# Dividing by the softmax sum after the product with v for eight tiles, with the sums from TensorE, and a new order of the first stage

## The chip, the cores and the metric

The kernel runs on one core of one Trainium2 chip. The metric is the device time of one execution in microseconds (us), as the median of three runs. Engines are called by the profile's names: PE is TensorE's matmul side and PEld its weight loads, DVE is VectorE, ACT is ScalarE, POOL is GpSimd, SP is SyncE, which issues nearly all DMAs.

## What is computed

Attention inside chunks of 64 tokens, for 8 batches of 8 heads, 576 tokens and 64 elements per head, then two feed-forward blocks over the 4608 tokens:

```python
scores = scale * np.matmul(q_c, k_c.transpose(0, 1, 2, 4, 3))     # q_c, k_c, v_c: chunks of 64 tokens
scores = scores - np.max(scores, axis=-1, keepdims=True)
attn = np.exp(scores)
attn = attn / (np.sum(attn, axis=-1, keepdims=True) + 1e-09)
out = np.matmul(attn, v_c)
...
xn = x / rms * rms_g                       # x: 4608 tokens x 512
g = xn @ w_gate                            # 512 x 1536
silu = g * (1.0 / (1.0 + np.exp(-g)))
val = xn @ w_val
x = silu * val @ w_out                     # 1536 x 512
h = x @ w_in                               # 512 x 2048
out = (h * np.cos(h)) @ w_out              # 2048 x 512
```

## The kernel before

The program has four stages: attention with the first four blocks of 128 gate and value columns, the other gate and value columns, the first output product with the second block's first product, and the last product. From the second stage on a product of blocks is made from seven smaller ones; nothing of that is touched. All large products run in three passes on values split into a high half and a low half (`mm3`, line 293).

The change is in the first stage. It takes 36 tiles of 128 tokens (all 8 heads of two chunks), two tiles to a unit. What each engine does, in which order, is written out by hand as a string of step names, `ORDER`; an engine executes its own steps in exactly the order of the string and waits where a step's input or buffer isn't there yet. The first letter names the step and the number the tile (or the unit, for s and v):

- s (sx for the second tile): PE makes the scores of a unit, 32 products on 64x64 quarters of the array, line 401 or 418. m: DVE takes row maxima (433, 435). b: DVE subtracts them (447, 450). e: ACT takes the exponential in place (454).
- n: DVE sums the rows (459), adds 1e-9 (460) and takes the reciprocal (461). z: the tile is multiplied by it (469), by POOL for tiles 0 and 1 as a step of its own, by DVE at the end of n for all others.
- t: PE transposes the tile (476). c: ACT copies it to SBUF (481). v: PE multiplies by v for a unit (492), again 32 products on 64x64 quarters, with the transposed tile as the weights.
- r: ACT sums squares (506). w: POOL makes the factor (511, 513). y: DVE scales (517). x: PE transposes (525). j: ACT makes the high half (534). a: ACT copies (539). l: the low half, by POOL for tiles 0 and 1 (545), by DVE for others (547).
- D: SP loads a block of gate or value weights, which come as 64-bit floats. k (ACT), p and q (DVE, lines 122, 123 and 127, 128), H (ACT) and L (POOL) turn it into high and low halves; k20 is block 2 of the gate weights, k21 of the value weights. Steps with a leading P do the same for weights of the second stage.
- gA2: the gate product of token chunk A (256 tokens, tiles 0 and 1; B is tiles 2 and 3) with weight block 2, 12 matmuls of 256 columns; vA2 the value product; S is ACT's silu, h DVE's multiplication, Y the store.

PSUM has eight banks: four under the tag `at` (scores, transposed tiles, product with v), in turn, and four under `gv` (gate and value products, and the scores of units 1 and 3). A step that takes a bank waits until the readers of the step four banks back in that ring are through.

Of the kernel before, what the change touches and what calls it, by code (L numbers as in the profile page):

```python
# [9 lines left out]
F32 = mybir.dt.float32  # L10
# [10 lines left out]
P = 128  # L21
# [19 lines left out]
POOL_Z = 2  # L41
POOL_L = 2
# [40 lines left out]
def kernel(  # L83
# [275 lines left out]
    with ExitStack() as st:  # L359
# [10 lines left out]
        unit, pair = {}, {}  # L370

        def load_qk(n):
            t = wp.tile([P, 2, NHP, P], F32, tag=f"p{22 + n % 4}", name="qk")
            nc.sync.dma_start(out=t, in_=qk[n])
            unit[n] = {"qk": t}

        def load_v(n):

            vt = ap_.tile([P, D], F32, tag="v", name="v", bufs=4)
            if n % 2:  # L380
                nc.sync.dma_start(out=vt[HD:, :], in_=v[n * P : n * P + HD, :])
                nc.sync.dma_start(out=vt[:HD, :], in_=v[n * P + HD : (n + 1) * P, :])
            else:
                nc.sync.dma_start(out=vt, in_=v[n * P : (n + 1) * P, :])
            unit[n]["v"] = vt
# [70 lines left out]
        def unit_n(n):  # L456
            p = unit[n]["p"]
# [8 lines left out]
        def unit_z(n):  # L466
            p, z = unit[n]["p"], unit[n].pop("z")
# [15 lines left out]
        def att_v(u):  # L483
            for b in range(2):
                unit[u + b]["o"] = bank("o")
            for hp in range(NHP):
                for h in range(2):
                    for b in range(2):
                        s = unit[u + b]
                        for c in range(2):  # L490
# [7 lines left out]
                            )  # L498
            for b in range(2):
                unit[u + b].pop("pts"), unit[u + b].pop("v")  # L500

        def unit_r(n):
# [3 lines left out]
            nc.scalar.activation(s["xn"], s["o"], AF.Square, accum_out=s["ss"])  # L506
# [143 lines left out]
        def step(name):  # L650
# [19 lines left out]
            D00 Q0 s0 k00 p00 Q1 q00 m0 Q2 Q3 sx V0 b0 H00 e0 I Pl0 s1 V1 m1 b1 e1 n0 n1 L00 z0 t0 D01 m2 Pa0 z1 m3 c0 b2 b3  # L670
            Q4 Dg e2 t1 Pb0 c1 Q5 D20 k01 e3 v0 V2 r1 n2 r0 w1 p01 n3 y1 w0 V3 t2 t3 c2 y0 s2 q01 Pc0 c3 k20 m4 D21 Q6 x0 m5
            a0 j0 b4 Pd0 e4 b5 x1 n4 l0 v1 e5 j1 a1 Q7 r3 n5 r2 t4 w3 V4 Pl1 V5 t5 w2 c5 p20 D31 Pa1 k21 c4 Q8 D11 y3 y2 s3
            q20 x2 x3 D10 H20 H01 m6 j2 v2 l1 m7 gA0 j3 L01 L20 b6 e6 r5 r4 b7 l2 l3 n6 w4 e7 a2 Q9 k11 Pl2 SA0 w5 y4 p21
            Q10 n7 V6 k10 gB0 vA0 vB0 SB0 t6 q21 a3 gB2 t7 c6 X0 V7 H21 x4 Pb1 hB0 y5 hA0 gA2 L21 c7 j4 s4 Pc1 x5 vB2 Ph0 V8
            l4 SB2 k31 m8 vA2 SA2 j5 m9 b8 a4 hB2 b9 YB0 v3 l5 gC2 gC0 p10 p11 e8 vC2 q10 a5 YA0 D30 Q11 e9 V9 X2 q11 H10
            Po0 hA2 k30 SC2 SC0 Pd1 L10 X1 V10 r6 Q12 w6 vC0 Pa2 Pk0 n9 n8 p30 r7 gB1 t9 y6 H11 w7 c9 y7 gA1 hC0 t8 c8 hC2
            q30 L11 SB1 Pl3 p31 H30 x6 s5 j6 Q13 L30 YB2 x7 m10 SA1 a6 l6 j7 b10 vA1 V11 vB1 q31 Ph1 YC0 hB1 hA1 l7 m11 b11
            gC1 e10 YA1 v4 r8 H31 n10 Po1 r9 w8 e11 y8 vC1 gB3 gA3 n11 w9 SC1 L31 y9 SB3 hC1 t10 vA3 a7 t11 Pb2 s6 SA3 c11
            vB3 m12 gC3 c10 x8 m13 x9 V12 Q14 YA2 b12 e12 b13 V13 YC2 X3 YB1 hA3 Pk1 Pc2 v5 j8 l8 hB3 e13 j9 r10 n13 a8 gD0
            gD1 Q15 r11 Pl4 l9 n12 SC3 a9 Pd2 X4 t13 V14 Q16 w11 y11 w10 vC3 vD1 Pa4 c13 y10 t12 SD0 s7 hC3 c12 SD1 Pb4 m15  # L680
            m14 b14 x10 j10 l10 b15 x11 vD0 hD1 hD0 Ph2 gD3 v6 gD2 e14 a10 e15 n14 Po2 j11 r12 r13 YA3 w13 vD3 w12 SD3 V15
            Q17 YC1 vD2 a11 n15 t15 l11 y13 y12 t14 Pa3 c15 s8 SD2 c14 Pc4 m16 b16 m17 b17 hD3 x12 x13 gE0 a12 e16 j12 n16
            v7 l12 Pb3 gE1 e17 t16 vE0 j13 n17 r14 a13 r15 c16 Pd4 l13 w14 SE0 Pk2 Q18 Ph4 t17 w15 c17 Q19 y15 y14 Pc3 hD2
            Q20 V16 V17 X5 Pl5 s9 x14 m19 m18 b18 Po4 b19 j14 x15 SE1 j15 l15 Pd3 gE2 v8 a14 e19 hE0 n19 l14 Pa5 V18 r17 Pk4
            Pl6 vE1 vE2 e18 Q21 r16 X6 n18 Pb5 V19 Ph3 SE2 a15 w16 y16 w17 y17 gE3 hE2 hE1 t19 c19 t18 X7 V20 Q22 c18 SE3
            s10 Q23 Pc5 m20 m21 Po3 b20 b21 e20 e21 Pa6 gF0 x16 a16 Pk3 vE3 x17 v9 a17 YE1 j16 W8 Pl7 r18 w18 Q24 n21 r19
            SF0 w19 j17 l16 n20 y19 hE3 l17 y18 Pd5 gF2 vF0 t21 t20 Ph5 s11 SF2 c20 c21 vF2 Pb6 x18 m22 b22 Pc6 hF0 Po5 m23
            x19 gF3 e22 Q25 Pk5 Pa7 b23 V21 v10 vF3 gF1 n22 Pd6 Ph6 a18 Po6 r20 e23 Pl8 Pb7 n23 hF2 a19 j18 r21 Pk6 w20 j19
# [12 lines left out]
            YI3 V35 e34 Pb15 v16 r32 gJ2 Po14 w32 YD1 e35 SJ2 r33 n34 n35 y32 t34 vJ2 w33 t35 Pk14 c34 SJ0 vJ0 hJ2 y33 Pc15
# [658 lines left out]
```

## Time and profile before

| | us |
|---|---|
| median of three runs (1628.81 to 1628.98) | 1628.95 |
| the profiled execution, its own time | 1627.73 |
| its span, first to last instruction | 1625.9 |
| PE busy | 1601.7 |
| DVE busy | 1362.5 |
| ACT busy | 954.2 |
| POOL busy | 235.0 |

The profile is one execution, and times inside it count from the start of the span. PE counts as busy from the start of a matmul to its modelled end. The first stage's last value product ends at 303.69, where the first matmul of the second stage starts.

### The profile page before, as it was taken

What the parts mean: (1) busy time and instruction counts of PE and PEld (TensorE: products, weight loads), DVE (VectorE), ACT (ScalarE), POOL (GpSimd) and SP (SyncE); (2) the same over time, 40 slices, a digit from 0 to 9 for tenths busy, and PEclk for the clock granted to TensorE, in tenths of its full rate; (3) what the DMA queues carried; (4) which work ended last, traced back from release to release, by engine and by line L of the source; (5) the groups of instructions that cost most, each with busy time, mean ns of one, the idle gap of its engine ahead of it and who ended that gap; (6) DMA issues with size and microseconds to landing.
All of it is one profiled execution on the core that took longest, in us unless ns stands there. A gap on an engine that the chain in (4) does not pass through costs nothing.

```text
span 1625.9 us, 29179 instructions
## 1 busy us (share of the span) xinstructions
PE 1601.7 (99%) x11208; PEld 1555.1 (96%) x11208; DVE 1362.5 (84%) x1862; ACT 954.2 (59%) x1378; POOL 235.0 (14%) x276
## 2 busy tenths in 40 slices
PE   6999999999999999999999999999999999999998
PEld 5998888899999999999999999999999999999998
DVE  8988775588988886889999689988989977877876
ACT  5786765354655554445555478887888634444443
POOL 3434442022223221001112000000000000000000
PEclk9999999999999999999999999999999999999999
DMA  9668996797767778786677864433433665346331
GB/s 333 220 219 264 337 330 230 272 325 250 241 221 250 242 229 270 290 261 201 208 246 243 303 250 144 149 132 131 146 125 119 230 211 167 96 126 185 107 100 38
DMA packets 293130, 342.97 MB, mean 211 GB/s; under 512 B 87936, under 2 KB 265600, under 8 KB 292992
## 3 DMA queue, kind: packets, MB, share of 16 engines
q1 hardware_dynamic: 292192, 341.02, 64.2%
q8 instruction: 88, 1.44, 0.4%
q14 instruction: 50, 0.41, 0.1%
q10 hardware_dynamic: 800, 0.10, 0.0%
HBM read 197.92 MB, written 143.13 MB: 210 GB/s over the span
## 4 chain that ended last, share of the span: by engine, by line
PE 73%; DVE 2%; issue 0%; DMA 0%; SPq 0%; ACT 0%; DVEq 0%; ACTq 0%
PE b L293 73%; DVE z L808 0%; DMA q<-xd 0%; DVE xt L357 0%; DVE wraw L198 0%; DVE z L819 0%; DVE q L339 0%; DVE wt L127 0%; DVE sg L819 0%; DMA out_dram<-o 0%; ACT z L804 0%; DVE wt L128 0%; SPq L827 0%; DVE wt L123 0%; SPq L1247 0%
## 5 line engine op out<-in xcount | busy, mean ns | idle before, releaser
L293 PE MATMUL b<-xo,w 128*128 128x384 f32 x3528 | 612.9, 334 | 0.0
L293 PEld LDWEIGHTS b<-xo,w 128*128 128x128 f32 x3528 | 611.4, 188 | 1.2 <-ACT xo L280 0.7
L293 PE MATMUL b<-xt,w 128*128 128x384 f32 x1728 | 306.1, 335 | 2.4 <-ACT z L804 0.9
L293 PEld LDWEIGHTS b<-xt,w 128*128 128x128 f32 x1728 | 299.5, 188 | 5.5 <-ACT z L804 2.0
L293 PE MATMUL b<-x,w 128*128 128x384 f32 x1440 | 261.9, 334 | 0.2 <-DVE z L808 0.2
L293 PEld LDWEIGHTS b<-x,w 128*128 128x128 f32 x1440 | 250.3, 188 | 1.4 <-DVE z L808 0.6
L280 ACT CAST xo<-q 128x768 fp32r<-128x768 f32 x144 | 118.3, 836 | 117.6 <-PE b L293 97.7
L281 DVE TENSOR_TENSOR xo<-q,xo 128x768 fp32r<-128x768 f32 x144 | 135.1, 952 | 53.3 <-ACT xo L280 53.1
L293 PE MATMUL b<-q,w 128*128 128x384 f32 x864 | 157.7, 334 | 0.0
L293 PEld LDWEIGHTS b<-q,w 128*128 128x128 f32 x864 | 150.5, 188 | 0.0
L251 POOL TENSOR_TENSOR wout<-wt,wout 128x384 fp32r<-128x384 f32 x44 | 55.4, 1258 | 435.2 <-ACT wout L249 316.6
L861 ACT CAST xo<-rawh 128x768 fp32r<-128x768 f32 x98 | 80.0, 837 | 57.2 <-PE b L293 28.3
L804 ACT COPY z<-b 128x768 f32<-128x768 f32 x72 | 57.4, 798 | 87.5 <-PE b L293 68.7
L293 PE MATMUL v<-xt,w 128*128 128x512 f32 (+1 forms) x528 | 108.2, 357 | 0.0
L293 PE MATMUL g<-xt,w 128*128 128x512 f32 (+1 forms) x528 | 107.5, 355 | 0.0
L866 DVE TENSOR_TENSOR xo<-rawh,xo 128x768 fp32r<-128x768 f32 x98 | 95.9, 1012 | 3.2 <-ACT xo L861 3.1
L293 PEld LDWEIGHTS g<-xt,w 128*128 128x128 f32 x528 | 85.8, 189 | 13.1
L293 PEld LDWEIGHTS v<-xt,w 128*128 128x128 f32 x528 | 85.1, 189 | 13.0
L808 DVE TENSOR_TENSOR z<-b,z 128x768 f32<-128x768 f32 x72 | 68.3, 951 | 31.8 <-PE b L293 21.3
L949 DVE TENSOR_TENSOR u<-b,z 128x768 f32<-128x768 f32 x72 | 68.2, 951 | 15.6 <-ACT z L944 12.7
L969 DVE SCALAR_TENSOR_TENSOR q<-q,u 128x768 f32<-128x768 f32 x72 | 68.4, 952 | 10.7 <-ACT q L967 10.2
L959 DVE SCALAR_TENSOR_TENSOR q<-q,u 128x768 f32<-128x768 int32 x72 | 68.1, 952 | 10.0 <-ACT q L955 9.8
(139 smaller groups left out, 2059.4 us busy)
## 6 DMA issues: line engine op xcount, KB each, us to landing
wraw<-in_w_dram SPq DMA_DIRECT2D x240, 128.0 KB, 3.5
gd<-q SPq DMA_DIRECT2D x80, 384.0 KB, 2.5
q<-gd SPq DMA_DIRECT2D x80, 384.0 KB, 3.9
rawh<-hd SPq DMA_DIRECT2D x66, 384.0 KB, 5.4
w<-kout SPq DMA_DIRECT2D x49, 512.0 KB, 6.2
qk<-in_qk_dram SPq DMA_DIRECT2D x36, 512.0 KB, 6.2
kgv<-wout SPq DMA_DIRECT2D x16, 896.0 KB, 5.8
w<-kgv SPq DMA_DIRECT2D x28, 512.0 KB, 6.9
```

The costliest lines, as they stand in the source:

```text
L251: nc.gpsimd.tensor_tensor(b[n][:, :, 1], a, f32(b[n][:, :, 0]), op=ALU.subtract)
L280: nc.scalar.copy(hi, a)
L281: nc.vector.tensor_tensor(lo, a, f32(hi), op=ALU.subtract)
L293: nc.tensor.matmul(acc, a, b, start=first and k == 0 and q == 0, stop=k == n - 1 and q == 2, skip_group_check=True)
L804: nc.scalar.copy(sums[s, g, k], z[s, g, "b1"])
L808: nc.vector.tensor_tensor(t, z[s, g, "b2" if k == 0 else "b5"], t, op=ALU.add)
L861: nc.scalar.copy(to[0], source2(s, g, j))
L866: nc.vector.tensor_tensor(to[1], source2(s, g, j), f32(to[0]), op=ALU.subtract)
L949: nc.vector.tensor_tensor(t, acc, part, op=ALU.add)
L959: nc.vector.scalar_tensor_tensor(q, k, -1.0, u, op0=ALU.mult, op1=ALU.add)
L969: nc.vector.scalar_tensor_tensor(q, q, -PI2, u, op0=ALU.add, op1=ALU.mult)
```

## The change

For tiles 0 to 7 (`SUMS = 8`) the exponential goes to PE undivided. Beside each of the 32 products of a unit with v stands a second one with the same weights and a column of ones, 64x1, into one of two extra PSUM banks of the ring `gv`; it gives the row sums. n then only adds 1e-9 and takes the reciprocal, reading the sums from PSUM; z, now a step of its own on DVE, multiplies the product with v by it, from PSUM into the SBUF buffer of the exponential, and r and y read that buffer. POOL no longer divides tiles 0 and 1 nor makes their low halves (`POOL_Z`, `POOL_L`); DVE does both. `ORDER` is new from its first to its last line.

```diff
-POOL_Z = 2
-POOL_L = 2
+POOL_Z = 0
+SUMS = 8
...
+        ones = tp.tile([P, 1], F32, tag="ones", name="ones")
+        nc.gpsimd.memset(ones, 1.0)
...
         def unit_n(n):
+            if n < SUMS:
+                z = unit[n]["z"] = sm.tile([P, NH], F32, tag="z", name="z")
+                nc.vector.tensor_scalar(z, pair["z"][n % 2], 1e-9, None, op0=ALU.add)
+                nc.vector.reciprocal(z, z)
+                return
...
         def unit_z(n):
+            if n < SUMS:
+                s = unit[n]
+                s["on"] = s.pop("pu")
+                z = s.pop("z").unsqueeze(2).to_broadcast([P, NH, HD])
+                nc.vector.tensor_tensor(s["on"], s.pop("o").rearrange("p (a b) -> p a b", b=HD), z, op=ALU.mult)
+                return
...
         def att_v(u):
+            if u < SUMS:
+                zt = pair["z"] = [ps_g.tile([P, D], F32, tag="gv", name="zt")[:, :NH] for _ in range(2)]
...
+                            if u < SUMS:
+                                nc.tensor.matmul(
+                                    zt[b][part(c), 2 * hp + h : 2 * hp + h + 1],
+                                    s["pts"][part(c ^ b), hp, part(h ^ b ^ (0 if u else c))],
+                                    ones[part(c ^ b), :],
+                                    start=True,
+                                    stop=True,
+                                )
...
-            if n < POOL_L:
-                a = pair["x", n // 2][:, :, cols(n, 2)]
-                nc.gpsimd.tensor_tensor(x[:, 1], a, f32(x[:, 0]), op=ALU.subtract)
-            else:
-                nc.vector.tensor_tensor(x[:, 1], unit[n]["tr"], f32(x[:, 0]), op=ALU.subtract)
+            nc.vector.tensor_tensor(x[:, 1], unit[n]["tr"], f32(x[:, 0]), op=ALU.subtract)
...
-            D00 Q0 s0 k00 p00 Q1 q00 m0 Q2 Q3 sx V0 b0 H00 e0 I Pl0 s1 V1 m1 b1 e1 n0 n1 L00 z0 t0 D01 m2 Pa0 z1 m3 c0 b2 b3
-            Q4 Dg e2 t1 Pb0 c1 Q5 D20 k01 e3 v0 V2 r1 n2 r0 w1 p01 n3 y1 w0 V3 t2 t3 c2 y0 s2 q01 Pc0 c3 k20 m4 D21 Q6 x0 m5
+            I D20 Q0 s0 Q1 m0 sx b0 m1 b1 Q2 Q3 e0 t0 k20 V0 p20 e1 V1 D01 t1 Q4 Dg c0 c1 s1 q20 H20 m2 b2 m3 k01 b3 Q5 v0
+            e2 e3 p01 n1 n0 z1 z0 r1 t3 t2 r0 q01 c3 c2 L20 w1 w0 y1 y0 s2 x1 m4 D21 k21 x0 H01 j0 V2 m5 b4 j1 V3 b5 p21 l1
```

PE, from the scores of unit 1 to the first gate and value products, before (sc scores, pt the transposed tile, o the product with v, tr the transposed scaled tile, g and v gate and value products):

```order
L418 MATMUL sc<-qk 64x64 x32
L476 MATMUL pt<-ident,p 128x128 x8
L492 MATMUL o<-v,pts 64x64 x32
L476 MATMUL pt<-ident,p 128x128 x8
L418 MATMUL sc<-qk 64x64 x32
L525 MATMUL tr<-ident,xn 128x128 x8
L492 MATMUL o<-v,pts 64x64 x32
L476 MATMUL pt<-ident,p 128x128 x8
L418 MATMUL sc<-qk 64x64 x32
L525 MATMUL tr<-ident,xn 128x128 x8
L492 MATMUL o<-v,pts 64x64 x32
L293 MATMUL g<-xt,w 128x256 x24
```

The same queue now, from the first transposes, with the first rows of the first product with v (zt are the sums):

```order
L489 MATMUL pt<-ident,p 128x128 x8
L420 MATMUL sc<-qk 64x64 x32
L507 MATMUL o<-v,pts 64x64
L515 MATMUL zt<-ones,pts 64x1
L507 MATMUL o<-v,pts 64x64
L515 MATMUL zt<-ones,pts 64x1
```

and where the first gate product stands, right behind the second unit's product with v:

```order
L515 MATMUL zt<-ones,pts 64x1
L293 MATMUL g<-xt,w 128x256 x12
L489 MATMUL pt<-ident,p 128x128 x8
L420 MATMUL sc<-qk 64x64 x32
L550 MATMUL tr<-ident,xn 128x128 x8
```

The first gate product stood behind three units' products with v, and now stands behind two, alone; the transposes of unit 0 moved ahead of the scores of unit 1; and every product with v of the first four units has a one-column product behind each of its 32.

DVE, before, between the row maxima of tile 1 and the division of tile 2:

```order
L433 TENSOR_REDUCE mx<-sc 128x4 x2
L447 TENSOR_TENSOR p<-sc,mx 128x4x64 x2
L459 TENSOR_REDUCE z<-p 128x8
L460 TENSOR_SCALAR z<-z 128x8
L461 RECIPROCAL z<-z 128x8
L459 TENSOR_REDUCE z<-p 128x8
L460 TENSOR_SCALAR z<-z 128x8
L461 RECIPROCAL z<-z 128x8
L435 TENSOR_REDUCE mx<-sc 128x8 x2
L450 TENSOR_TENSOR p<-sc,mx 128x512 x2
L122 TENSOR_SCALAR wt<-wt 128x512
L123 TENSOR_SCALAR wt<-wt 128x512
```

and now, from the same place on:

```order
L435 TENSOR_REDUCE mx<-sc 128x4 x2
L449 TENSOR_TENSOR p<-sc,mx 128x4x64 x2
L122 TENSOR_SCALAR t<-t 128x512
L123 TENSOR_SCALAR t<-t 128x512
L127 SCALAR_TENSOR_TENSOR t<-raw,t 128x512
L128 SCALAR_TENSOR_TENSOR t<-raw,t 128x512
L437 TENSOR_REDUCE mx<-sc 128x8
L452 TENSOR_TENSOR p<-sc,mx 128x512
L437 TENSOR_REDUCE mx<-sc 128x8
L452 TENSOR_TENSOR p<-sc,mx 128x512
```

The row sums of tiles 0 and 1 are gone from here, and the first conversion of weights (block 2), which stood ahead of the first row maximum with block 0, comes behind the subtraction of tile 1. What DVE does with the sums now stands behind the product with v:

```order
L461 TENSOR_SCALAR z<-zt 128x8
L462 RECIPROCAL z<-z 128x8
L461 TENSOR_SCALAR z<-zt 128x8
L462 RECIPROCAL z<-z 128x8
L478 TENSOR_TENSOR p<-o,z 128x512 x2
```

The addition, the reciprocal and the division of both tiles follow each other; no reduction is left.

## Rows read from the trace of the kernel before

**Rows 1.** The page's first part: busy us, share of span, instructions.
```profile
PE 1601.7 (99%) x11208; PEld 1555.1 (96%) x11208; DVE 1362.5 (84%) x1862; ACT 954.2 (59%) x1378; POOL 235.0 (14%) x276
```
**Rows 2.** Busy time by stretch: start:end length, engines in turn, granted clock, DMA share, GB/s.
```profile
10.00:38.12 28.12, 19.36 (x420) 15.74 (x420) 27.21 (x57) 16.96 (x34) 11.91 (x18) 0.94 1.03 340
...
54.13:303.69 249.56, 248.63 (x2921) 212.09 (x2922) 187.90 (x339) 160.08 (x294) 91.80 (x150) 1.00 0.82 272
```
**Rows 3.** What PE waited for, 0 to 38: us in total, times, longest.
```profile
PE sc L401 <- DMA qk<-in_qk_dram: 5.7, 1, 5.7
PE pt L476 <- DVE p L469: 4.1, 3, 1.5
```
**Rows 4.** The same wait list, 38 to 80, then 80 to 320.
```profile
PE pt L476 <- DVE p L469: 0.9, 2, 0.6
...
PE b L293 <- DVE xt L357: 0.6, 1, 0.6
```
**Rows 5.** PE in order of time: start, us, operation, count.
```profile
5.67 1.14 PE L401 MATMUL sc<-qk 64*64 64x64 f32 x32 [5.67 <-DMA qk<-in_qk_dram]
...
16.21 0.48 PE L492 MATMUL o<-v,pts 64*64 64x64 f32 x4
...
32.70 1.99 PE L418 MATMUL sc<-qk 64*64 64x64 f32 x64
...
38.12 3.13 PE L293 MATMUL g<-xt,w 128*128 128x256 f32 x24
41.09 3.04 PE L293 MATMUL v<-xt,w 128*128 128x256 f32 x24
```
**Rows 6.** The granted clock while the third score product ran, columns as in rows 2.
```profile
32.00:34.00 2.00, 2.00 (x52) 1.67 (x54) 2.00 (x4) 1.13 (x3) 1.54 (x2) 0.50 0.99 385
```
**Rows 7.** PE, the fourth unit's product with v, and the next matmul.
```profile
52.79 1.34 PE L492 MATMUL o<-v,pts 64*64 64x64 f32 x64
...
54.06 3.14 PE L293 MATMUL g<-xt,w 128*128 128x256 f32 x24
```
**Rows 8.** DVE in order of time, first subtractions; then 30 to 39.
```profile
9.36 0.76 DVE L447 TENSOR_TENSOR p<-sc,mx 128x256 f32<-128x256 f32 x2 [1.25 <-PE sc L401]
...
11.35 0.67 DVE L459 TENSOR_REDUCE z<-p 128x8 f32<-128x512 f32 x1
...
29.70 0.68 DVE L459 TENSOR_REDUCE z<-p 128x8 f32<-128x512 f32 x1
30.41 0.17 DVE L460 TENSOR_SCALAR z<-z 128x8 f32<-128x8 f32 x1
...
30.85 0.69 DVE L469 TENSOR_TENSOR p<-p,z 128x512 f32<-128x512 f32 x1
31.46 0.42 DVE L122 TENSOR_SCALAR t<-t 128x512 f32<-128x512 f32 x1
...
32.26 1.40 DVE L517 SCALAR_TENSOR_TENSOR xn<-o,rs,gamma 128x512 f32<-128x512 f32 x2
33.58 0.68 DVE L127 SCALAR_TENSOR_TENSOR t<-raw,t 128x512 uint32<-128x512 uint32 x1
...
34.90 1.28 DVE L435 TENSOR_REDUCE mx<-sc 128x8 f32<-128x512 f32 x2
36.10 1.28 DVE L450 TENSOR_TENSOR p<-sc,mx 128x512 f32<-128x512 f32 x2
37.30 1.27 DVE L547 TENSOR_TENSOR xt<-tr,xt 128x512 fp32r<-128x512 f32 x2
38.49 0.67 DVE L459 TENSOR_REDUCE z<-p 128x8 f32<-128x512 f32 x1
```
**Rows 9.** PE in order of time, once it is dense.
```profile
83.53 1.03 PE L525 MATMUL tr<-ident,xn 128*128 128x128 f32 x8
84.49 1.16 PE L492 MATMUL o<-v,pts 64*64 64x64 f32 x64
85.58 3.14 PE L293 MATMUL g<-xt,w 128*128 128x256 f32 x24
```

More of the change, by code (lines that the diff above doesn't have):

```diff
@@ L374, in load_qk @@
             nc.sync.dma_start(out=t, in_=qk[n])
-            unit[n] = {"qk": t}
+            unit.setdefault(n, {})["qk"] = t
         def load_v(n):
@@ L384, in load_v @@
                 nc.sync.dma_start(out=vt, in_=v[n * P : (n + 1) * P, :])
-            unit[n]["v"] = vt
+            unit.setdefault(n, {})["v"] = vt
         def part(h):
@@ L674 @@
[L674 to L688, printed above, removed]
@@ new lines @@
+            Pl0 D00 Q6 e4 v1 l0 q21 L01 n2 e5 a0 k00 gA2 a1 Q7 V4 n3 z2 t5 r2 Pa0 p00 z3 r3 t4 w2 q00 c4 SA2 c5 s3 w3 H00 y2
+            H21 y3 Pb0 L21 x2 Pc0 m6 x3 j2 V5 v2 b6 vA2 j3 m7 L00 b7 gA0 D10 D11 Q8 l2 n4 l3 n5 a2 k10 hA2 z5 a3 e7 Q9 e6 X0
+            k11 Pl1 V6 gB2 t6 z4 r5 p11 p10 q11 r4 c6 SA0 vB2 Pd0 w5 y5 w4 t7 s4 gB0 vA0 c7 y4 q10 m9 m8 SB2 hB2 Ph0 H10 x4
+            Pa1 j4 x5 b8 V7 b9 Po0 D30 hA0 j5 V8 D31 SB0 k30 e9 vB0 e8 l5 l4 L10 hB0 p30 H11 k31 v3 gC0 L11 gC2 Q10 YA2 n6
@@ new lines @@
+            n12 hB3 Q17 v5 j9 YB1 e13 Pd2 r11 n13 l9 vD2 r10 w10 w11 y11 gD3 SD2 a9 Pa4 t12 y10 Pb4 hD2 gD1 Pc4 SD3 t13 vD3
+            c12 SD1 s7 m14 x10 vD1 b14 Ph2 c13 Po2 j10 m15 hD3 x11 gC3 Pk2 b15 e14 Pa3 a10 e15 l10 Pd4 v6 V14 n14 r12 j11
+            a11 n15 gD0 l11 vC3 w12 r13 t14 hD1 y12 V15 w13 t15 y13 c14 SC3 Pb3 vD0 s8 x12 Ph4 Pc3 X4 j12 c15 m16 SD0 m17
+            gE0 b16 e16 b17 x13 YA3 a12 l12 v7 n16 hC3 e17 r14 vE0 r15 a13 j13 t16 w15 V16 Q18 SE0 gE1 n17 w14 y15 l13 t17
+            Q19 V17 y14 c16 s9 x14 hD0 Po4 c17 m18 X5 b18 m19 a14 j14 Pl5 b19 V18 hE0 x15 vE1 X6 Q20 v8 j15 Pa5 V19 gE2 e18
@@ new lines @@
+            Q21 YC3 a15 e19 Pb5 r16 r17 Pd3 w16 Pk4 SE1 w17 l15 n18 l14 YD2 Pl6 hE1 Q22 n19 gE3 t18 vE2 y16 t19 c18 y17 SE2
+            Ph3 V20 Po3 s10 c19 Q23 m20 Pc5 vE3 b20 m21 hE2 Pa6 b21 Pd5 SE3 V21 e20 e21 YE1 Pl7 x16 x17 Pb6 gF0 j16 v9 Pc6
+            j17 a16 l16 gF2 r19 SF0 r18 Q24 Pk3 n20 t20 hE3 l17 n21 a17 vF0 w19 w18 y18 Q25 c20 X7 Ph5 Po5 X8 y19 t21 x18
+            Pa7 c21 s11 m22 vF2 Pd6 V22 Pk5 W8 x19 b22 Q26 hF0 Pb7 m23 a18 j18 j19 a19 V23 gF1 Pl8 X9 SF2 W9 b23 l18 e23 v10
+            e22 r20 r21 Ph6 w20 w21 Po6 l19 Pc7 n23 n22 gF3 SF1 y20 t23 Pd7 Pk6 vF1 Pa8 YD1 t22 hF2 y21 s12 c22 m24 c23 m25
@@ new lines @@
+            b28 a24 YG1 j24 SH2 c27 x25 hG3 l24 Pc10 b29 Q30 j25 e28 a25 vH2 v13 Pd10 Ph10 r27 n28 vH3 t28 Q31 e29 r26 V28
+            gH0 Pl11 w27 Pl12 w26 l25 n29 Pa12 W11 Po10 y27 y26 Pb12 t29 c28 W12 Q32 Pk10 SH3 s15 V29 W13 c29 hH2 m30 x26
+            Pc12 m31 Pa11 SH0 Pd12 gH1 x27 j26 j27 vH0 hH3 b30 b31 Pb11 l26 v14 Ph12 Q33 e31 a26 l27 Po12 YG3 a27 Pc11 e30
+            SH1 gI2 r29 vH1 hH0 SI2 X12 V30 Pd11 r28 n30 w29 w28 t30 c30 n31 vI2 y28 y29 Q34 YH3 t31 Pl13 Pk12 hI2 hH1 s16
+            x28 m33 gI3 V31 c31 j28 Pa13 a28 m32 x29 Ph11 l28 b32 Pl14 b33 Pb13 vI3 e32 j29 Pc13 v15 e33 gI0 n32 n33 l29 gI1
@@ new lines @@
+            r30 Po11 SI3 Pa14 r31 w30 Pd13 V32 w31 t33 hI3 y30 a29 X14 vI0 t32 Q35 SI0 x30 Pk11 V33 Pl15 X13 Pb14 c33 Ph13
+            Pc14 y31 Po13 c32 s17 W14 Pd14 j30 SI1 hI0 YD0 m35 Pk13 YH1 a30 V34 x31 vI1 j31 l30 m34 a31 X15 Pa15 b34 l31 v16
+            Pb15 b35 r33 gJ2 w33 r32 Ph14 e35 w32 e34 Pc15 W19 gJ3 hI1 y32 n34 vJ2 n35 t34 Po14 SJ2 y33 vJ3 SJ3 Pd15 t35
+            Pk14 c34 c35 hJ2 Ph15 gJ0 x32 x33 Po15 V35 v17 SJ0 a32 j32 r34 hJ3 r35 W20 j33 a33 X16 w35 w34 W21 YI3 vJ0 l32
+            YI1 gJ1 Pk15 SJ1 l33 hJ0 y34 y35 x34 j34 l34 x35 a34 j35 l35 vJ1 gK2 hJ1 gK0 vK2 a35 X17 Z W15 W16 SK2 YJ3 gK1
@@ L705 @@
+            gK3 W17 W18 hK2 SK0 vK0 O1 YJ1 SK1 vK1 O2 vK3 hK0 SK3 hK1 hK3 YK1 YK3
             """
```

36 lines of the change are left out of this document (14 added, 22 removed).

## The prediction

> **What bounds the kernel now.** I read the page's first part, then busy time by stretch, then what PE waited for, then PE and DVE in order of time. PE is busy for 99% of the span [rows 1], so only time in which PE stands or works slowly can be won. It lies almost wholly ahead of 38.12, where the first gate product starts [rows 5]: of the 28.1 us before it PE is busy for 19.4, DVE for 27.2, that is 97% [rows 2]. There PE waits 5.7 us for the first scores' data and 4.1 us for DVE's division by the softmax sum [rows 3]. So DVE's queue sets when the first gate products can run. From 38 on PE is dense: 0.9 us of waiting up to 80, 0.6 us from there to 320 [rows 4], and between 54.13 and 303.69 it is busy for 248.6 of 249.6 us while DVE has 62 us to spare [rows 2]. What the change can bring or cost is decided in the first 54 us.
>
> PE's clock matters too. 64 passes of a score product take 1.99 us at 32.70 [rows 5], where the granted clock is 0.50, 1.2 GHz [rows 6]; the same number of passes takes 1.09 us (84.49 to 85.58, [rows 9]) at 2.4 GHz. The first scores, 64-wide too, run at the slow figure: 1.14 us for 32 passes [rows 5]. I count PE's early steps as slow until about 25, an estimate: up to 38 PE stands for a third of the time [rows 2], and that is where the slow figures are.
>
> **A point at which both orders can be compared.** When the product with v of unit 3 is over, both orders have put the same steps through PE: the scores of units 0 to 4, the transposes of tiles 0 to 7, four products with v, the second transposes of tiles 0 to 5, and eight gate or value products of 256 columns (A and B with blocks 0 and 2). Before, that is at 54.06 [rows 7]. I work out when it is now.
>
> **DVE's queue.** DVE's prices, as distances between starts [rows 8]: a maximum, a subtraction or a low half 0.60 (two start 1.20 apart); a division 0.61; a scaling 0.66; the two halves of a conversion 0.80 and 1.32, so 2.12 in all; addition and reciprocal 0.44; the reduction that goes away 0.71; the half-size operations of tiles 0 and 1 0.66 each. The low half reads PSUM and the division before reads SBUF, at 0.60 and 0.61, so I leave the division at 0.61 though it now reads PSUM, and the scaling at 0.66.
>
> The change removes eight reductions from DVE (8 x 0.71 = 5.7 us) and gives it two divisions and two low halves that POOL had (2.4 us): 3.3 us less. It also defers the conversions, so that the low halves of tiles 0 and 1, for which gA2 waits, come sooner. But the point that binds is the low half of tile 3, for gB2, after which PE has enough work to stay dense. Ahead of it DVE now has: five conversions (blocks 20, 01, 21, 00 and one for the second stage) 10.6; the eight half-size operations of tiles 0 and 1 2.7; six maxima and six subtractions 7.2; five additions with reciprocals 2.2; four divisions 2.4; four scalings 2.6; four low halves 2.4. That is 30.1 us. The first maximum can start when the first scores are there, at 6.9 (5.67 + 1.14, [rows 5]); before, DVE filled the time up to then with a conversion, now it stands.
>
> Without a gap the low half of tile 3 would be ready at 37.0. I find three gaps by walking the queues. The first subtraction waits for the second tile's scores, which wait for the first maximum: 1.25 us, as before [rows 8]. Then tile 1's subtraction ends at 10.8, its exponential at about 11.5 (one operation of that size), its transposes take 1.0 (0.48 at full clock, [rows 9], twice) and the scores of unit 1 behind them 2.0, with handovers until 14.7; DVE is through with conversion 20 at 13.0 and stands for 1.7. The product with v of unit 0 follows at 2.0, and its sums at a price I come to, until 18.7; DVE reaches them at 17.9 and stands for 0.8. Later products with v come in time (unit 1's ends about 28.1, DVE wants its sums at 29.1). Together 3.7 us: **the low half of tile 3 ends at 40.8**, gB2 starts at 40.9. By then PE has run gA2, vA2 and gA0, which hide under DVE.
>
> **PE from there.** Behind gB2's start lie five products at 1.49 (24 matmuls start 2.97 apart, [rows 5]), 7.4; two sets of transposes and two of second transposes at 0.48 and the scores of unit 4 and the product with v at 1.09 [rows 9], 4.1; the sums of unit 3. For two places where ACT comes late (the transposes of tile 6 wait for an exponential behind a change of function table, the extra banks of unit 3 for a silu) I add 0.9, the size of the waits that PE had at such places [rows 4].
>
> **The sums' price.** No row shows a product with one column. Per unit there are 32 more, with the same 64 columns of weights to load and two passes each. Below, the price is nothing: the four quarters of the array work side by side. Nearest is the product with v itself, 1.09 us for 64 passes [rows 9], and I take that, 1.1 (2.0 at the slow clock). Above: each product with v and its sum sit on the same quarter. If the next quarter can't start until that sum has, the four no longer overlap. 64 passes in 1.09 us, four at a time, is 0.068 a round; one quarter after the other 64 passes take 4.4 us, against my 2.2 for product and sum. Two passes per product do already follow each other on one quarter, and four passes, two products, took 0.48 us at the slow clock [rows 5], with the next product still held back. In single file, at 0.124 a round (1.99 by 16), the fourth would start 0.37 after the first, which leaves it less than a round. So a second pass that has to wait doesn't hold up the next quarter, which speaks for the low price; that the queue sees past two more entries, no row shows.
>
> The Trainium skill says in "TensorE: Matmul & The Clock Gate", Part 3, that a weight load overlaps running matmuls only if its row group differs, and that matmuls start strictly in order. By that rule the sum, on its own product's row group, would hold up what follows, and the kernel would come out near the first rival's time. The row at 16.21 disagrees in part.
>
> **The sum.** 40.9 + 7.4 + 4.1 + 1.1 + 0.9 = 54.4, against 54.06: 0.3 us later. Behind that point PE's work is the same, and DVE's about the same: it is ahead by a few conversions and behind by the sums and divisions of tiles 6 and 7, within 1 us of the 188 it does up to 303.69 [rows 2]. So I leave the 0.9 us that PE waited before, and pass 0.3 on to the end: 1627.73 + 0.3 = 1628.0 for the profiled execution, which lies 1.2 below the median of 1628.95. **Forecast: 1629.3 us**, no difference that a measurement of this kernel can tell (about 0.2%, 3.3 us).
>
> **Rivals.**
> - *The sums go single file* (slower). Unit 0's product, at the slow clock, takes 8.0 us (64 x 0.124) in place of 4.0, and DVE waits 4.0 longer for the sums; units 1 and 2 add 2.2 each, of which about 1 is covered (DVE comes 1 us after unit 1's end; PE waits for a bank at gA0); unit 3 adds 2.2. Together 8.6: 1637.9, and 1633 to 1637 if the overlap goes in part. It decides from about 1 us a unit more than I take: 1.8 at unit 0's slow clock, 1.0 at unit 3, little at the two that are covered, with my 0.3 the 3.3 us that can be told. For it: the sums stand singly between the products. Against it: the 0.48 us row. Chance 0.25.
> - *DVE's gaps close* (faster). If PE's clock is up by 12, the scores of unit 1 and the first product with v cost half, and 2.5 us of gaps go; with them the 0.9 of ACT's lateness and the 0.9 that PE waited later: -4.3 + 0.3, 1625.0. Against it: PE still stands for as large a share of that time, and DVE's gap at the first subtraction stays. Chance 0.14.
> - *The later order is worse* (slower). All units up to 303 are reordered; six new waits like the longest of 0.6 [rows 4] make 4 us: 1633. Chance 0.07.
> - *It does nothing*: after 80 PE once waits 0.6 us for DVE [rows 4], which can swallow so small a shift; that lies inside the forecast.
>
> **How the numbers follow.** The forecast has 0.54, its own range is 1626 to 1632. Faster by over 0.2% is the second rival, 0.14; slower is the first and third, 0.32. The range for 8 in 10 goes from 1625.5 to 1637.5; it leaves out the full first rival and more than the second gives.
>
> **What would show it.** First gate product at about 28 instead of 38.12, but gB2 only near 41; the matmul behind the fourth product with v near 54.5; the product with v and its sums at about 2.2 us at full clock. A product with v over 3.5 us means the first rival. DVE without its gaps at 13 and 18 means the second. A chain that is over 2 us ahead or behind at 54, or new waits of PE beyond 60, make the forecast wrong.

## The result and the profile after

| | us |
|---|---|
| median of four runs after (1648.65 to 1650.72) | 1649.57 |
| median before, on the same chip | 1628.88 |
| ratio after to before, 95% interval | 1.0129 (1.0117 to 1.0140) |
| the profiled execution after, and its span | 1649.19, 1647.4 |
| PE busy, DVE busy (before in [rows 1]) | 1614.5, 1360.5 |

The change makes the kernel 20.7 us slower; 1629.3 had been forecast, with a range up to 1637.5. The profiled span is 21.5 us longer. PE's busy time is 12.8 us longer than in [rows 1], so more than half of the loss is not idle time but work that is added or slower. Where it arises is read first from PE in order of time (start, us, operation, count, the wait before it in brackets):

```profile
18.79 0.41 PE L507 MATMUL o<-v,pts 64*64 64x64 f32 x4 [2.51 <-issue]
...
29.05 0.53 PE L507 MATMUL o<-v,pts 64*64 64x64 f32 x3 [0.67 <-PE tr L550]
...
33.16 0.80 PE L293 MATMUL g<-xt,w 128*128 128x256 f32 x2
35.81 2.50 PE L293 MATMUL g<-xt,w 128*128 128x256 f32 x10 [1.86 <-POOL ms L535]
...
46.13 3.04 PE L293 MATMUL g<-xt,w 128*128 128x256 f32 x24
...
60.54 1.22 PE L293 MATMUL g<-xt,w 128*128 128x256 f32 x8
...
262.38 1.11 PE L550 MATMUL tr<-ident,xn 128*128 128x128 f32 x4 [2.96 <-ACT pts L494]
263.14 5.08 PE L293 MATMUL v<-xt,w 128*128 128x512 f32 x12
...
278.09 3.02 PE L293 MATMUL v<-xt,w 128*128 128x512 f32 x12
...
297.24 1.94 PE L550 MATMUL tr<-ident,xn 128*128 128x128 f32 x8 [5.30 <-DVE xn L542]
298.83 4.34 PE L293 MATMUL v<-xt,w 128*128 128x512 f32 x12
...
324.77 6.86 PE L293 MATMUL b<-xt,w 128*128 128x384 f32 x37
```

Two points can be compared. The matmul behind the fourth product with v (called the matched point below) starts at 60.54 against 54.06 [rows 7]: 6.5 us lost at the start. The second stage starts at 324.77 against 303.69: 21.1 us, so 14.6 more are lost inside the first stage; the rest of the kernel adds 0.4. The two waits near 262 and 297 are 8.3 us; behind each of them PE works at the slow clock (12 matmuls of 512 columns in 5.08 and 4.34 us, against 3.02 at 278, where PE is dense; the granted clock is 0.66 from 260 to 270 and 0.75 from 290 to 300).

Busy time by stretch (PE, PEld, DVE, ACT, POOL, then the granted clock, DMA share, GB/s):

```profile
10.00:20.00 10.00, 6.84 (x199) 6.05 (x200) 6.62 (x14) 5.04 (x9) 1.27 (x1) 0.92 1.05 337
20.00:30.00 10.00, 7.31 (x111) 6.06 (x109) 8.37 (x16) 4.94 (x12) 3.95 (x5) 0.50 0.97 295
30.00:40.00 10.00, 8.14 (x173) 7.66 (x170) 9.24 (x20) 4.55 (x11) 2.21 (x4) 0.55 0.90 302
...
6.85:45.51 38.66, 28.48 (x667) 25.36 (x668) 31.20 (x63) 20.02 (x39) 9.43 (x12) 0.74 0.89 290
240.00:250.00 10.00, 10.00 (x125) 8.15 (x115) 8.57 (x16) 7.50 (x13) 3.47 (x5) 1.00 0.20 61
...
280.00:290.00 10.00, 10.00 (x110) 8.31 (x109) 2.07 (x3) 5.31 (x12) 3.74 (x6) 1.00 0.20 65
290.00:300.00 10.00, 4.70 (x20) 3.87 (x19) 2.70 (x4) 1.48 (x3) 0.00 (x0) 0.75 0.96 311
```

DVE now stands for a third of the time from 10 to 20 (before, it was busy for 97% up to 38, [rows 2]), and the granted clock is 0.50 to 0.55 from 20 to 40, mostly the lower level, 1.2 GHz. Late in the stage there is a sign of another kind: from 240 to 250 and from 280 to 290 PE is dense, yet the DMA share is 0.20. Something may be holding back transfers; PE's waits follow, from 259.4 and from 291.9. A low share alone proves nothing: the kernel before has 0.27 from 270 to 280, with PE dense and no wait behind it:

```profile
270.00:280.00 10.00, 10.00 (x108) 8.24 (x107) 2.69 (x4) 5.43 (x14) 3.31 (x6) 1.00 0.27 92
```

After the change, SP's own list in order of time names the cause:

```profile
238.26 0.38 SPq L386 DMA_DIRECT2D v<-in_v_dram  x1
252.23 0.57 SPq L572 DMA_DIRECT2D xd<-xf  x1
252.85 0.62 SPq L376 DMA_DIRECT2D qk<-in_qk_dram  x1
253.56 0.91 SPq L204 DMA_DIRECT2D kgv<-wout  x1
...
277.84 0.67 SPq L166 DMA_DIRECT2D w<-kgv  x1
288.56 0.56 SPq L572 DMA_DIRECT2D xd<-xf  x1
...
289.89 1.47 SPq L629 DMA_DIRECT2D hd<-h  x2
```

SP issues nothing from 238.6 to 252.2 and from 278.5 to 288.6. Each time the next step is a store of transposed tiles (`xd<-xf`, X14 and X16), which waits for ACT's second copy into its buffer. ACT, around the first stand:

```profile
251.62 0.59 ACT L564 COPY xf<-tr 128x512 f32<-128x512 f32 x1
...
260.81 0.51 ACT L657 CAST wout<-wt 128x384 fp32r<-128x384 f32 x1 [6.17 <-DMA kgv<-wout]
```

and DVE behind the second:

```profile
295.74 0.69 DVE L625 TENSOR_TENSOR h<-sg,v 128x512 f32<-128x512 f32 x1 [6.48 <-DMA hd<-h]
```

The chains can be read off. X14 waits for the copy that ends at 252.2. Behind it on SP is the store Pk11 of prepared weights, which empties the only buffer `wout`. ACT's cast for the next weights waits 6.2 us for that buffer, and the copies that PE's transposes wait for stand behind it on ACT. In the second place YI3 and YI1 (`hd<-h`) stand behind X16. Their buffer is the one that DVE's next product needs; it waits 6.5 us, the scalings of tiles 34 and 35 are queued behind it, and PE waits for these.

### The profile page after: what moved, and what is told of

Read it like the earlier page. It is cut to its first block, busy times and chain, and to the rows that moved or that the text cites. A ratio compares the mean times of both kernels' runs of the same rounds, so it can differ in the third digit from the quotient of the medians.

```text
span 1647.4 us, 29711 instructions
## 1 busy us (share of the span) xinstructions
PE 1614.5 (98%) x11464; PEld 1566.3 (95%) x11464; DVE 1360.5 (83%) x1858; ACT 957.4 (58%) x1380; POOL 234.9 (14%) x273
## 4 chain that ended last, share of the span: by engine, by line
PE 72%; DVE 2%; issue 1%; DMA 0%; SPq 0%; ACT 0%; DVEq 0%; ACTq 0%
PE b L293 72%; DVE z L829 0%; DVE xt L357 0%; DMA q<-xd 0%; DVE wraw L198 0%; DVE q L339 0%; DVE sg L840 0%; DVE z L840 0%; DVE wt L127 0%; DMA out_dram<-o 0%; ACT z L825 0%; DVE wt L122 0%; DVE wt L128 0%; DVE q L337 0%; DVE wt L123 0%
## 5 line engine op out<-in xcount | busy, mean ns | idle before, releaser
L293 PE MATMUL v<-xt,w 128*128 128x512 f32 (+1 forms) x528 | 112.7, 365 | 0.0
```

Source lines behind the costliest of these rows:

```text
L293: nc.tensor.matmul(acc, a, b, start=first and k == 0 and q == 0, stop=k == n - 1 and q == 2, skip_group_check=True)
```

## Experiments on the late loss: SyncE's queue

In the first three kernels only SP's steps move. SP's sequence at the two places (V, Q, Pl and W load; X, Y and Pk store), the change (-) and the kernel with both moved (+):

```diff
- Pl14 V32 X14 Q35 Pk11 V33 Pl15 X13
+ Pl14 V32 Q35 Pk11 V33 Pl15 X13 X14
...
- V35 W20 X16 W21 YI3 YI1 Pk15
+ V35 W20 W21 YI3 YI1 X16 Pk15
```

**Both moves.**

> The changed kernel with two stores of transposed tiles moved back in SyncE's queue, nothing else: that of tiles 28 and 29 (X14) behind X13, so that the scores' data Q35, the kept weights Pk11, the values V33 and the raw weights Pl15 go ahead of it, and that of tiles 32 and 33 (X16) behind the two stores of h, YI3 and YI1. Theory (queue): some 14 us of the 21 lost lie between 238 and 320, where SyncE stands 12.5 us at X14 and 10.0 at X16 while those transfers wait behind them; the moves take both stalls away: 1634 to 1638. Rival (the new order of the other engines costs it): SyncE's stalls only go along with it, 1646 to 1650. In both the start up to 60 us stays 6 us late.

Measured: 1634.98, ratio to before 1.0038 (1.0024 to 1.0051): 14.6 us come back. SP in order of time:

```profile
245.72 0.57 SPq L204 DMA_DIRECT2D kgv<-wout  x1
...
272.73 0.94 SPq L629 DMA_DIRECT2D hd<-h  x2
282.66 0.57 SPq L572 DMA_DIRECT2D xd<-xf  x1
```

Pk11 goes at 245.7 instead of 253.6 and the stores of h at 272.7 instead of 289.9. The second store still waits until 282.7, but nothing that PE needs soon stands behind it. PE waits at neither place any more; the matched point and the start of the second stage:

```profile
60.94 1.34 PE L293 MATMUL g<-xt,w 128*128 128x256 f32 x9
...
311.45 6.86 PE L293 MATMUL b<-xt,w 128*128 128x384 f32 x37
```

**The first move alone** (first two lines of the diff).

> Only the first of the two moves: X14 behind X13. Theory (queue): PE's waits of 0.35 and 2.96 at 258 and 262 and the slower products behind them go, about 6 us: 1642 to 1645; the wait of 5.3 at 297 stays. Rival (other engines): 1648 to 1651.

Measured: 1643.39, 6.2 less than the change; the second wait is still there:

```profile
291.54 1.94 PE L550 MATMUL tr<-ident,xn 128*128 128x128 f32 x8 [5.55 <-DVE xn L542]
```

**The second move alone.**

> Only the second of the two moves: X16 behind YI3 and YI1. Theory (queue): DVE's wait of 6.5 for a buffer of h at 295.7 and PE's of 5.3 behind it go, with the slow products after it, about 7.5 us: 1641 to 1644; the waits at 258 and 262 stay. Rival (other engines): 1648 to 1651.

Measured: 1641.41, 8.2 less than the change; now the first wait is the one that stays:

```profile
262.63 1.11 PE L550 MATMUL tr<-ident,xn 128*128 128x128 f32 x4 [2.83 <-ACT pts L494]
```

6.2 and 8.2 add up to 14.4; both moves together gave 14.6. The two stands are the late loss. What else the new order costs behind the matched point is 0.9 us: 311.45 - 60.94 = 250.5, against 303.69 - 54.06 = 249.6 before.

**The same fault put into the kernel before.** Again only SP's sequence:

```diff
- X15 YI3 V35 YD1 Pk14 YB3 YI1 YD2 X16
+ X15 V35 YD1 Pk14 YB3 YD2 X16 YI3 YI1
```

> The kernel before with one thing of the new order: the stores of h, YI3 and YI1, behind the store X16 in SyncE's queue. Theory (queue): X16 is issued at 276.1, so YI3 lands near 279, VectorE's product hJ0 waits for its buffer until then in place of 268.2, the scalings of tiles 34 and 35 come behind it at 280 to 281, and their transposes, due at 278.3, wait 2 us or more, with products at the slow clock behind: 1630.5 to 1635. Rival (only the changed kernel's other engines make that place tight): 1628 to 1629.

Measured: 1634.05, ratio 1.0037 (1.0024 to 1.0049): 5.8 us slower. PE in order of time:

```profile
283.01 1.97 PE L525 MATMUL tr<-ident,xn 128*128 128x128 f32 x8 [3.75 <-DVE xn L517]
284.63 3.71 PE L293 MATMUL v<-xt,w 128*128 128x512 f32 x12
```

A wait of 3.75 us, then a product at the slow clock: the same picture in a kernel with none of the new computation.

## Experiments on the start

With the stores moved, 6.4 us are left. I tried to divide them between the products with ones, the division behind the product with v, and the stands of PE that the profile marks `issue`.

**The new computation in the old order.** The table of steps is the old one, save n and z:

```diff
- ... n0 n1 ... z0 ... z1 ... v0 V2 r1 n2 r0 ...
+ ... v0 V2 n1 z1 n0 z0 r1 r0 ...
```

> The new computation in the old order: the row sums of tiles 0 to 7 by products with ones, the division behind the product with v, but every step where the old kernel has it, save the sums' additions and divisions, which stand just ahead of the squares that need them (VectorE does the divisions and low halves of tiles 0 and 1, as in the changed kernel). Theory (order): what the new order does to SyncE's queue behind 238 us isn't there, and VectorE's queue is shorter than before at the start, while TensorE's instructions for the sums can make it stand once or twice at the start (2.5 and 1.9 us in the changed kernel): 1626 to 1634. Rival (the computation itself costs it): the sums and the later division cost the 6 us that are lost up to 60 us in any order: 1635 or more.

Measured: 1639.49, ratio 1.0066 (1.0054 to 1.0079). The rival holds: in the old order the new computation costs 10.9 us, more than in the new order with its stores moved.

**The products with ones left out.** In the kernel with both stores moved:

```diff
-                            if u < SUMS:
-                                nc.tensor.matmul(
...
-                nc.vector.tensor_scalar(z, pair["z"][n % 2], 1e-9, None, op0=ALU.add)
+                nc.vector.tensor_scalar(z, unit[n]["mz"], 1e-9, None, op0=ALU.add)
```

> The kernel with both stores moved, with the products with ones left out: the additions of tiles 0 to 7 read the row maxima in place of the sums, so the softmax division of these tiles is by something else; steps, order and VectorE's work stay. Theory (sums): the 6 us still lost at the start come from the products with ones, which lengthen the product with v by 2 us at the slow clock and 1.1 at the full one, and double its instructions, so that TensorE stands for its own code at 16.3: the stand of 3.2 us goes, 1628 to 1631. Rival (late division): the loss comes from what now stands behind the product with v on VectorE, whoever makes the sums: 1633 to 1636.

Measured: 1633.06, ratio 1.0028 (1.0018 to 1.0039). By the medians 1.9 us come back, the rival's lower end; the interval overlaps that of the kernel with the products (1.0024 to 1.0051), so the times alone don't tell it from nothing. The traces show where the rest goes. The stand of 3.2 us is gone, and the first value product starts 4.3 us sooner (39.73 against 44.07). Then PE waits 1.4 us for DVE and 1.7 for ACT, the granted clock falls, and at the matched point only 0.7 us is left (60.28 against 60.94). From 45 to 50, without the products and with them:

```profile
45.00:50.00 5.00, 3.34 (x20) 3.14 (x19) 2.90 (x7) 4.97 (x11) 0.99 (x3) 0.67 0.80 231
...
45.00:50.00 5.00, 4.57 (x39) 4.37 (x39) 2.87 (x10) 4.88 (x8) 2.39 (x5) 1.00 0.89 286
```

So this pair of runs gives no clean price of the products in this order.

**The sums by VectorE's reductions, division still late.**

```diff
+                nc.vector.tensor_reduce(z, unit[n].get("p", unit[n].get("pu")), axis=AX.X, op=ALU.add)
```

> The kernel with both stores moved, with the row sums of tiles 0 to 7 by VectorE's reductions again (eight of 0.71, just ahead of each product with v), the division still behind it; no products with ones. Theory (sums): most of the loss at the start goes, less what the reductions take where VectorE has no gap: 1628 to 1632. Rival (late division): 1634 to 1638.

Measured: 1639.99, ratio 1.0071 (1.0058 to 1.0084). Worse than either expectation, and 5.0 worse than with the products. I read it so that in this order DVE has no place for eight reductions: the products with ones spare DVE more than they cost PE.

**The old order, only the division late** (the same reduction line; z just ahead of r, n where it was).

> The old order with the division alone moved behind the product with v, the reductions on VectorE where they were; no products with ones. To be set beside the old order with products (1639.5) and the kernel before (1628.6). Theory (sums): 1629 to 1633, so that most of the 10.9 between those two is the products' price. Rival (late division): 1636 to 1640, so that most of it is the division's.

Measured: 1632.96, ratio 1.0026 (1.0016 to 1.0035), inside the first theory's range. In the old order the late division costs 4.5 us; that includes the divisions and low halves of tiles 0 and 1, which DVE now does in POOL's place. What PE waited for there, 0 to 61:

```profile
PE tr L539 <- DVE xn L531: 4.0, 2, 2.1
PE o L504 <- issue: 3.8, 2, 3.3
```

Before, PE never waited for the scaled tile (`xn`) in that stretch; its waits for DVE were for the divided tile [rows 3]. The division has only changed sides: the same two DVE steps now stand between the product with v and the second transposes. The 3.3 us that the profile calls `issue` are DVE's too. They end at 27.63, 0.1 us after DVE's subtraction of tile 4 (the first of the two in the first line here, over at 27.53) has freed the scores' bank that this product writes:

```profile
26.85 1.27 DVE L450 TENSOR_TENSOR p<-sc,mx 128x512 f32<-128x512 f32 x2
...
27.63 2.57 PE L504 MATMUL o<-v,pts 64*64 64x64 f32 x64 [3.34 <-issue]
```

**The products alone, unused, in the kernel before.**

```diff
+            zt = [ps_g.tile([P, D], F32, tag="gv", name="zt")[:, :NH] for _ in range(2)]
...
+                                nc.tensor.matmul(
+                                    zt[b][part(c), 2 * hp + h : 2 * hp + h + 1],
```

> The kernel before with the 256 products with ones added to its first four products with v, into banks that nobody reads; all else, its reductions and divisions too, stays. The products' price by itself. Theory (sums): 2 us each for the two at the slow clock, 1.1 each for the two at the full one, and a stand for code: 1632 to 1637. Rival (late division): the products fit into time in which TensorE waits for VectorE anyway: 1628 to 1630.

Measured: 1631.88, ratio 1.0018 (1.0009 to 1.0027): 3.4 us, just below the range given. (These are 128 products of two passes each: 256 passes, not 256 products.) With 4.5 for the division that makes 7.9, while both together cost 10.9 in the old order. That both delay the same chain is how I read it; it was not tried further.

**The same in the first two units only** (`if u < 4`).

> The kernel before with the unused products with ones in its first two products with v alone, 128 in place of 256 (all four: 1631.9). Theory A (they hide while TensorE waits for VectorE's queue, up to 38 us): 1628 to 1629.3, and the 3.4 us come from the third and fourth product. Theory B (they delay the first chains at the slow clock): 1630.3 to 1631.5.

Measured: 1629.76, ratio 1.0007 (0.9998 to 1.0016). This is 1.4 us more than before, lies between the two expectations and can't be told from nothing. Inconclusive.

**The low halves of tiles 0 and 1 back on GpSimd**, in the old order with the late division:

```diff
+            if n < 2:
+                a = pair["x", n // 2][:, :, cols(n, 2)]
+                nc.gpsimd.tensor_tensor(x[:, 1], a, f32(x[:, 0]), op=ALU.subtract)
```

> The old order with the late division and VectorE's reductions (1633.0), but the low halves of tiles 0 and 1 on GpSimd again, as in the kernel before. Theory (VectorE's queue): the loss of 4.5 is mostly the four operations of 0.6 that came from GpSimd to VectorE, which bounds the start in this order; two of them gone give about 1.2 back: 1631 to 1632.3. Rival (the chain behind the product): 1632.7 to 1634.

Measured: 1632.36, ratio 1.0026 (1.0017 to 1.0035), between the two ranges. Some 0.6 of the 4.5 us is the low halves that DVE took over, if any; the intervals overlap. What the two divisions that came from POOL cost was not tried.

**The new order with the old computation** (reductions and divisions ahead of the transposes, both stores moved):

```diff
- ... e0 t0 k20 V0 p20 e1 V1 D01 t1 ... p01 n1 n0 z1 z0 r1 t3 t2 r0 ...
+ ... e0 k20 V0 p20 n0 z0 t0 e1 V1 D01 n1 z1 t1 ... p01 r1 n3 t3 n2 t2 r0 ...
```

> The old computation in the new order with both stores moved: reductions and divisions of tiles 0 to 7 ahead of their transposes again (the divisions of tiles 0 and 1 on GpSimd, as before), no products with ones. To be set beside 1635.0 for the same order with the new computation. Theory A (the new computation costs it, the order gains): 1626 to 1629. Theory B (the order itself costs part of the start's 6 us, whatever is computed): 1631 to 1636.

Measured: 1644.11, ratio 1.0095 (1.0080 to 1.0111), 9 us worse than the same order with the new computation and beyond both theories. PE's waits, 0 to 61:

```profile
PE pt L476 <- DVE p L469: 13.8, 6, 4.1
...
PE pt L476 <- POOL p L469: 5.8, 2, 5.2
```

So the new order, with the steps placed as here, suits the new computation alone. Each half by itself (1639.5 and 1644.1) is worse than both together (1635.0), and both together still lose against the old pair.

**PE's own instructions.** The stand of 2.51 us at 16.3 lies inside the first product with v and has no releaser. While it lasts, one piece of instruction code comes in. The DMA queues from 16 to 18 (packets, MB, share of 16 engines), after the change:

```profile
q1 hardware_dynamic: 299, 0.77, 100.9%
q8 instruction: 1, 0.02, 3.3%
```

and from 35 to 37 in the kernel before, just ahead of its only such stand (0.99 us, up to 37.73):

```profile
q1 hardware_dynamic: 423, 0.73, 99.8%
q8 instruction: 1, 0.02, 3.1%
```

After the change the whole run has 90 such pieces for 2 x 11464 records of PE and PEld, 255 a piece: 128 passes with their weight loads, which is why I take this queue for PE's. The Trainium skill says in "Runtime: NRT & Kernel Launch", Instruction fetch mechanics, that code comes in blocks of 16 KiB, 256 instructions, and that crossing into the next one is mostly hidden. The count agrees. "Mostly hidden" agrees for all but a few of the 90 pieces; at the places here it doesn't hold. Counted in the traces, the stands of 0.9 us or more that I put down to code come ahead of the 222nd and 475th pass after the change and the 474th before: about two pieces apart, whatever the program has there. Each ends 1.2 to 1.3 us after its piece has come in (after the change the pieces are in at 17.5 and 34.5, the stands end at 18.79 and 35.81; before, 36.5 and 37.73). The `issue` of 3.3 us in the old order with the late division is not of this kind: it lies ahead of the 281st pass, and the last piece before its end had been in for 3.3 us. To test whether the stands are code I shifted the stream by idle products of a zeroed tile ahead of the first scores:

```diff
+                if name == "N":
+                    warm = ps_g.tile([P, D], F32, tag="gv", name="warm")
+                    for k in range(64):
+                        p = slice(k % 2 * HD, (k % 2 + 1) * HD)
+                        nc.tensor.matmul(warm[p, :1], nil[p, :HD], nil[p, HD:], start=True, stop=True)
```

> The kernel with both stores moved, with 64 products of a zeroed tile (64 by 64 by 1) ahead of the first scores, while TensorE waits for data: the same work otherwise, but every later instruction of TensorE is 128 records further on in its stream. Theory (code): the stands of 3.2 us in the first product with v and 0.8 in the first gate product are waits for TensorE's own instructions, which are fetched in pieces of 16 KB; with the stream shifted, the pieces are asked for at other places, those two stands go, and 1 to 4 us are won: 1631 to 1634. Rival (those stands are waits for a transfer or a bank that the profile doesn't name): they stay where they are: 1634.5 to 1636.

> The kernel before with the same 64 idle products ahead of its first scores. Theory (code): its stand of 0.99 us at 36.7 goes, at the place that sets the first gate product: 1627 to 1628. Rival: no change, 1628 to 1629; if the idle products delay the first scores, more.

Measured: 1637.33, ratio 1.0056 (1.0043 to 1.0068), and 1630.29, ratio 1.0012 (1.0003 to 1.0021). The shift failed to move anything. A product of this kind is two passes, so 64 of them are 256 records, exactly one piece, and every border fell where it had been; besides they took 6.9 us and held up the first scores by 1.9 us (7.57 against 5.6 to 5.7), which came out at the end, 2.3 and 2.0. The stand of 2.5 us is still there in the changed kernel (up to 21.59), so idle products by themselves don't take it away. With 32 of them, half a piece (`range(32)`):

> The kernel with both stores moved, with 32 idle products (64 passes, 128 records of TensorE's stream) ahead of the first scores, half as many as in the run before, which shifted the stream by 256 records, just one piece of 16 KB, and delayed the first scores by 2 us. These 64 passes are over by about 4.4 us, ahead of the first scores. Theory (code): with a shift of half a piece the stands of 2.5 to 3.2 us in the first product with v and 0.8 to 1.9 in the first gate product go or turn up 128 records earlier in the program, where TensorE waits anyway; VectorE's wait for the sums shrinks: 1631.5 to 1634. Rival (a transfer or a bank): the stands stay at the same instructions: 1634.5 to 1636.

> The kernel before with the same 32 idle products ahead of its first scores. Theory (code): its stand of 0.99 us at 36.7 goes: 1627 to 1628. Rival: 1628.2 to 1629.

Measured for the changed kernel with both stores moved: 1632.89, ratio 1.0029 (1.0018 to 1.0041), 2.1 us better than without by the medians; the intervals overlap (1.0024 to 1.0051 without), so the traces have to decide. Its two stands, PE in order of time, without the shift:

```profile
19.52 0.41 PE L507 MATMUL o<-v,pts 64*64 64x64 f32 x4 [3.20 <-issue]
...
35.45 2.50 PE L293 MATMUL g<-xt,w 128*128 128x256 f32 x10 [0.76 <-issue]
```

and what there is with it:

```profile
21.44 1.03 PE L422 MATMUL sc<-qk 64*64 64x64 f32 x52 [1.03 <-issue]
...
58.04 3.14 PE L293 MATMUL g<-xt,w 128*128 128x256 f32 x24
```

Both are gone, one of 1.0 us has come up in other scores, ahead of the 349th pass (127 behind the 222nd), and the matched point is at 58.04, 2.9 us sooner. (A second `issue`, 1.12 us at 26.89, is the wait for DVE's subtraction again, which ends at 26.79; without the shift it is 0.93 at the same place.) The stand in the first gate product, which the profile of the change put down to POOL (`ms`), is `issue` in the same kernel with the stores moved, and goes with the shift: it was code too. The clock differs with the stand as well. Busy time by stretch, after the change and then with the shift:

```profile
18.00:20.00 2.00, 1.22 (x42) 1.21 (x42) 0.33 (x1) 0.20 (x1) 0.00 (x0) 0.61 1.08 253
20.00:25.00 5.00, 4.35 (x82) 3.85 (x78) 3.81 (x9) 3.36 (x8) 2.35 (x4) 0.50 0.95 307
...
18.00:20.00 2.00, 1.42 (x12) 1.08 (x12) 1.93 (x8) 0.70 (x3) 0.00 (x0) 1.00 1.07 256
20.00:25.00 5.00, 2.00 (x64) 1.52 (x64) 3.80 (x6) 2.82 (x8) 3.94 (x5) 1.00 0.91 278
```

In both the granted clock is 1.00 from 16 to 18. After the stand of 2.5 us it falls to the lower level; without it, it stays up until 25. For the kernel before with the shift: 1627.91, ratio 0.9998 (0.9989 to 1.0007). Its stand of 0.99 is gone from the trace, but no difference in time can be told. No version I ran beats the kernel before.

## Why the prediction was wrong

**The step that failed first** is "Behind that point PE's work is the same ... and pass 0.3 on to the end." PE's work is the same, but the order behind 54 us is another, and I compared only PE and DVE there. SP's queue was not walked past the first stage's start. Two stores stand ahead of steps that others wait for: 14.6 us, shown by moving them back, and the same fault costs the kernel before 5.8. The third rival ("The later order is worse", 0.07) had the right place, but the wrong mechanism and size: six waits of 0.6, priced from the longest wait of a dense stretch, in place of two stands of 12.5 and 10.0 us (by SP's wait list) on a queue that carries seven kinds of transfers there.

**The start** was 6.2 us worse than worked out, in these terms:
- *DVE's work*: 30.1 us forecast; 31.2 busy from 6.85 to the end of tile 3's low half. About right; 1.0 of the difference is one scaling of 1.74 us. (The price "0.66 each" of the half-size operations is for two of them, and the sum uses it so.)
- *DVE's gaps*: 3.7 forecast; 38.66 - 31.20 = 7.5 measured. The first two gaps came as worked out (1.3 and 1.5 against 1.25 and 1.7). The third, for the first sums, was 2.0 instead of 0.8, by PE's stand for code. A fourth kind was missed: DVE waits for POOL's factor ahead of three scalings (0.45 to 0.72 each).
- *The low half of tile 3*: ends at 45.5 instead of 40.8. gB2, the second half of the 24 matmuls at 46.13, starts about 47.6 instead of 40.9; PE itself was late by then. From there to the matched point it is 12.9 us against 13.5: that sum held.
- *PE's clock*: slow until "about 25" was an estimate from PE's share of standing. The granted clock is 1.00 up to 18 (though the scores at 12.78 still take the slow 1.99 us for 64 passes), and falls behind the stand for code: 0.61 from 18 to 20, 0.50 to 0.55 from 20 to 40. From 25 on it is low where I had it high, and the first gate products are at 33.16 instead of 28.
- *PE's code*: the one row that showed it, the old kernel's 0.99 `issue`, was not priced. Taking the two stands away brings the matched point 2.9 us forward, and the end 2.1 by the medians.

**What held.** The price of the sums: the second product with v and its sums take 4.1 us at the slow clock (29.05 to 33.16; 4.0 forecast). So the single-file rival fell, which wanted 8.0 there; the two later ones, at the full clock and without their waits, take 2.4 against my 2.2. The Trainium skill's rule in "TensorE: Matmul & The Clock Gate", Part 3, on weight loads of the same row group would have meant the single file, as the prediction applied it; the trace disagrees with that for this pattern. The products' 3.4 us in the old kernel do not speak against that price: the forecast put little beyond unit 3's 1.1 us on PE's path, and by this run more of the price lies there; how much each unit adds was not settled.

**What stays open.** 4.5 us of the start are left with stores and stream repaired, and their cause is not shown. The runs show that the late division costs about as much in the old order (4.5, or 3.9 with the low halves on POOL), and the trace there shows where PE waits. How much of it would be left in the new order without the slow clock was not tried: no experiment changed the clock alone.

## What to carry to other kernels

Where a hand-written order changes, walk every queue over the whole reordered stretch, the DMA issuer's first: a store that waits for its data stops all that stands behind it, and a kernel with single or few buffers turns that into stalls of compute engines later (here SP stood from 238.6 and 278.5, and PE from 259.4 and 291.9). A low DMA share while PE is dense is a reason to read the issuer's list, not a proof. Moving an operation from ahead of a product to behind it need shorten nothing if the chain through the same engine stays as long; look at which wait replaces the one removed, and, where the profile says `issue`, at what else ends at that moment.

## What was not expected of the hardware

- PE waits for its own instructions where many small products run in a row while the DMA engines are full: 2.51 us (3.20 in the next run) in a stretch with a DMA share of 1.05, at borders 128 passes apart. In both runs the granted clock fell behind the stand (0.61 and 0.52 from 18 to 20). Half a piece of idle products, which hide in time PE waits anyway, moved the borders.
- A second scaling on DVE took 1.74 us instead of 0.75 (at 25.41) while POOL made a weight's low half beside it (25.34 to 26.60, 1.26 us), and 1.74 us stand in seven other runs of this order.
- Added up from separate runs, the late division and the products cost 7.9 us; together they cost 10.9.
